# Out product of block 0 by pairs of token groups, and unit 2's and unit 3's attention steps moved ahead by one or two ff tiles

## The chip, the cores and the metric

One core of one Trainium2 chip. The metric is the device time of one execution in microseconds (us). The record calls a time slow when it is over 1.5% above the fastest of its kernel. Times inside an execution are read from its profile; they count from the start of the span, which is about 1.8 us shorter than the device time.

## The reference

Attention inside chunks of 64 tokens (8 batches, 8 heads, 576 tokens, head size 64), then a bilinear feed-forward product on the 4608 tokens that come out:

```python
scores = q_c @ k_c^T / sqrt(64)          # 64 x 64 per chunk and head
attn   = softmax(scores)
x      = (attn @ v_c)  -> [4608, 512]
out    = ((x @ w_a) * (x @ w_b)) @ w_out # d_ff = 1536
```

## The kernel before

The tokens are cut into 9 blocks of 512 and 18 units of 256. A block runs 12 "ff tiles" (eight matmuls into two PSUM banks, the buffers that TensorE writes to, a ScalarE copy, a VectorE product) and then an out product. The attention of the coming units is slipped between the matmuls of the running block: a *turn* (transpose of q and k), *scores*, an exponential, *sums* and values, a logarithm and inverse, and a *normalise* that writes the next block's input `xT`. The banks for the matmuls are a ring of four, `F`; attention uses `PS` and `PA`, of two banks each.

The out product of block 0 holds all four banks of the ring, one for each group of 128 tokens, and carries unit 2's attention:

```python
o = [nextF() for _ in range(4)]
for fts in [(ft,) for ft in range(NFT - 2)] + [(NFT - 2, NFT - 1)]:
    for tg in range(4):
        for ft in fts:
            out_products(tg, ft, o[tg])          # one matmul, N = 512
    if fts == (5,):   # turn of unit 2, on TensorE
        ...           # q evacuated by VectorE, k by ScalarE, both from PS
    if fts == (7,):
        scores(2, True); expo(2)
    if fts == (9,):
        sums(2, SU); values(2); log_sums(2, SU)
        for cl in range(2): inverse(2, cl); normalise(2, cl)
stores = [out_close(0, tg, o[tg], False, (V, A)[tg % 2]) for tg in range(4)]
```

Block 1 follows in two halves of 256 tokens (units 2 and 3). Units 4 and later are turned by a DMA transpose, issued by the sync engine in the order of the program, among loads and stores:

```python
turn_unit(4); load_unit(5, (1, 2))
for d in stores: store(*d)                       # block 0's output
load_unit(6, (0,))
for ft in range(10):                             # block 1, unit 2's half
    step(); ffn(1, ft, (0,))
    if ft == 1: turn_pairs(3, 0, (V,)); turn_pairs(3, 1, (A,))
    if ft == 3: slot(None, 3, True)              # scores of unit 3
    if ft == 5: slot(3, None, short=True)        # sums, ..., normalise of unit 3
cast_unit(5, (0,)); ...                          # GpSimd
turn_unit(5); load_unit(6, (1, 2)); load_unit(7, (0,))
for ft in range(10): step(); ffn(1, ft, (1,)); ...  # unit 3's half
...
for ft in range(10, NFT):
    step(); ffn(1, ft)
    if ft == 10: slot(4, 5)                      # sums of unit 4, scores of unit 5
```

`step()` runs what a slot left for later: exponential, inverse, normalise.

The softmax here doesn't subtract the row's maximum and nothing guards it: scores larger than these inputs give would overflow.

## Time and profile before

| | before |
|---|---|
| device time, median of the first 3 runs | 316.56 us |
| span of the profiled run | 314.3 us |
| TensorE / VectorE / ScalarE / GpSimd busy | 96 / 59 / 43 / 39% |
| first out matmul of block 0 | 37.41 us |
| block 1 starts | 52.34 us |
| scores of unit 5 | 75.55 us |

TensorE is the engine to watch, so what matters is where it stands still. The prediction shows its waits and its timeline. One more view, the busy time of each engine in a stretch of time, shows the hole that the change aims at (columns: the stretch, its length, then busy us and instructions of TensorE, weight loads, VectorE, ScalarE and GpSimd, the granted clock, the DMA share and GB/s):

```profile
50.60:52.30 1.70, 0.00 (x0) 0.00 (x0) 1.70 (x4) 1.25 (x3) 1.48 (x2) 1.00 0.99 223
```

For 1.70 us TensorE runs nothing at all, while VectorE works without a break: block 1 waits for VectorE.

### The profile page before, as it was taken

The page shows a single profiled execution, that of the slowest core. Times are in us where ns is not written, and L with a number is a line of the kernel's source. Part 1 is how long each engine was busy: PE and PEld are TensorE (multiplying, and loading weights), DVE is VectorE, ACT ScalarE, POOL GpSimd, SP SyncE. Part 2 cuts the span into 40 slices and gives each one's busy share as a digit, 9 for nine tenths or more (in the row PEclk, how much of TensorE's full clock was granted, in tenths as well). Part 3 has the DMA queues.
Part 4 walks back from the last instruction along what each step waited for, and adds up shares of the span by engine and source line. Part 5 has one row for each costly group of instructions (what it writes and reads, how often), then busy time and mean ns, then how long its engine had stood idle before and what let it go on. Part 6 is the DMA issues. An engine that isn't in the chain of part 4 may idle for free.

```text
span 314.3 us, 7318 instructions
## 1 busy us (share of the span) xinstructions
PE 300.9 (96%) x2891; PEld 177.9 (57%) x2924; DVE 184.4 (59%) x372; ACT 135.5 (43%) x233; POOL 124.1 (39%) x159
## 2 busy tenths in 40 slices
PE   7699997999999999999999999999999999999995
PEld 3444455876444476447644764467446744674474
DVE  3643314454447764967496749574967476646663
ACT  3822225846335542653265326441644164413320
POOL 2567958996384127402630164016500400040023
PEclk9999999999999999999999999999999999999998
DMA  7999999999999979998699239933500320020003
GB/s 262 267 316 385 372 296 260 218 302 234 224 221 284 228 158 266 238 184 188 198 251 220 68 136 204 265 71 135 134 2 2 84 53 1 2 100 36 0 1 136
DMA packets 146899, 55.01 MB, mean 175 GB/s; under 512 B 126256, under 2 KB 140848, under 8 KB 146864
## 3 DMA queue, kind: packets, MB, share of 16 engines
q1 hardware_dynamic: 145776, 53.49, 69.1%
q10 hardware_dynamic: 1088, 1.05, 1.0%
q8 instruction: 23, 0.38, 0.5%
q14 instruction: 12, 0.10, 0.1%
HBM read 37.75 MB, written 9.44 MB: 150 GB/s over the span
## 4 chain that ended last, share of the span: by engine, by line
PE 87%; DMA 4%; SPq 3%; DVE 2%; issue 1%; ACT 1%; POOL 1%; ACTq 0%; POOLq 0%; DVEq 0%
PE F L398 56%; PE F L479 19%; PE F L420 6%; SPq L154 2%; DMA wst<-in_moe_w_a_dram 2%; PE PS L234 2%; DMA f<-in_k_dram 2%; PE F L251 2%; PE PA L267 1%; SPq L147 1%; DVE xT L286 1%; DVE ab L410 0%; POOL part L497 0%; ACT qkT L167 0%; ACTq L140 0%
## 5 line engine op out<-in xcount | busy, mean ns | idle before, releaser
L398 PE MATMUL F<-xT,wb 128*128 128x512 bf16 (+1 forms) x443 | 110.4, 360 | 4.0 <-DVE osb L169 1.8
L398 PE MATMUL F<-xT,wa 128*128 128x512 bf16 (+1 forms) x472 | 112.9, 361 | 0.7 <-POOL wa L169 0.3
L409 ACT CAST bsb<-F 128x512 bf16<-128x512 f32 (+1 forms) x118 | 64.6, 548 | 106.0 <-PE F L398 105.7
L410 DVE TENSOR_TENSOR ab<-F,bsb 128x512 bf16<-128x512 f32 (+1 forms) x118 | 75.7, 643 | 54.7 <-PE F L398 46.4
L398 PEld LDWEIGHTS <-wa 128*128 128x128 bf16 x472 | 46.0, 98 | 48.2 <-POOL wa L169 1.4
L398 PEld LDWEIGHTS <-wb 128*128 128x128 bf16 x472 | 44.5, 98 | 46.5 <-issue 1.8
L497 POOL TENSOR_TENSOR part<-part 128x256 f32<-128x256 f32 x14 | 10.1, 724 | 133.7 <-ACT part L523 132.8
L169 POOL CAST qkb<-f 128x1024 bf16<-128x1024 f32 (+1 forms) x35 | 34.6, 1003 | 23.4 <-DMA f<-in_k_dram 13.4
L479 PEld LDWEIGHTS <-wst 128*128 128x128 bf16 x420 | 41.1, 98 | 4.8
L286 DVE TENSOR_TENSOR xT<-PA,inv 128x512 bf16<-128x512 f32 x32 | 21.8, 683 | 20.9 <-ACT inv L281 15.2
L479 PE MATMUL F<-wst 128*128 128x256 bf16 x252 | 33.3, 273 | 0.0
L497 DVE TENSOR_TENSOR osb<-F,part 128x256 f32<-128x256 f32 x56 | 22.3, 419 | 10.9 <-POOL part L497 9.4
L497 POOL TENSOR_TENSOR part<-part,osb 128x256 f32<-128x256 f32 x28 | 19.8, 727 | 11.5 <-DVE osb L497 11.4
L169 POOL CAST vb<-f 128x1024 bf16<-128x1024 f32 (+2 forms) x22 | 20.1, 918 | 7.1 <-DMA f<-in_v_dram 6.1
L479 PE MATMUL F<-wst,ab 128*128 128x256 bf16 x168 | 22.7, 273 | 0.0
L420 PE MATMUL F<-wo,ab 128*128 128x512 bf16 x92 | 21.3, 379 | 0.5 <-DVE ab L410 0.2
L468 DVE TENSOR_TENSOR wst<-ab 128x512 bf16<-128x512 bf16 x42 | 21.7, 517 | 0.0
L467 DVE TENSOR_TENSOR wst<-ab 128x512 bf16<-128x512 bf16 x42 | 20.9, 497 | 0.0
L277 ACT ACTIVATE lns<-F 128x512 f32<-128x512 f32 x30 | 16.3, 594 | 10.2 <-PE F L251 10.2
L479 PE MATMUL F<-wo,wst 128*128 128x256 bf16 x168 | 20.6, 273 | 0.0
L245 ACT ACTIVATE E<-PS 128x1024 bf16<-128x1024 f32 (+1 forms) x20 | 18.8, 942 | 3.7 <-PE PS L234 2.5
L497 DVE TENSOR_TENSOR part<-F,part 128x256 f32<-128x256 f32 x15 | 6.4, 425 | 21.3 <-POOL part L497 21.3
(58 smaller groups left out, 194.4 us busy)
## 6 DMA issues: line engine op xcount, KB each, us to landing
out_dram<-osb SPq DMA_DIRECT2D x31, 256.0 KB, 2.1
f<-in_q_dram SPq DMA_DIRECT2D x28, 256.0 KB, 4.3
f<-in_v_dram SPq DMA_DIRECT2D x28, 256.0 KB, 4.3
f<-in_k_dram SPq DMA_DIRECT2D x24, 256.0 KB, 3.9
wst<-in_moe_w_out_dram SPq DMA_DIRECT2D x6, 512.0 KB, 8.8
f<-in_v_dram SPq DMA_DIRECT2D x16, 128.0 KB, 3.3
wst<-in_moe_w_b_dram SPq DMA_DIRECT2D x4, 512.0 KB, 7.4
wst<-in_moe_w_a_dram SPq DMA_DIRECT2D x4, 512.0 KB, 8.2
```

The costliest lines, as they stand in the source:

```text
L169: eng.tensor_copy(out=out, in_=in_)
L245: nc.scalar.activation(out=e[:, :, s], in_=PS[:, :, s], func=AF.Exp, scale=scale)
L277: nc.scalar.activation(out=lns[:, cl, :], in_=SU[cl], func=AF.Ln)
L286: nc.vector.tensor_tensor(out=x.rearrange("p m (g c t) -> p c g m t", g=2, c=2)[:, cl], in0=PA[:, cl, :].rearrange(shape, g=2, m=4), in1=i ...
L398: nc.tensor.matmul(bank[:, 0:n], w[ft // 2][ft % 2][:, kt, :], x[:, kt, us[0] * 256:us[0] * 256 + n], start=(kt == 0), stop=(kt == NKT - 1),)
L409: nc.scalar.copy(out=bT[:, 0:n], in_=banks[0][:, 0:n])
L410: nc.vector.tensor_tensor(out=ab[ft][:, us[0] * 256:us[0] * 256 + n], in0=banks[1][:, 0:n], in1=bT[:, 0:n], op=MULT)
L420: nc.tensor.matmul(o, ab[ft][:, tg * 128:(tg + 1) * 128], wo[ft // 2][:, ft % 2, :], start=(ft == 0), stop=(ft == NFT - 1),)
L467: nc.vector.tensor_tensor(out=y[:, 0:2], in0=a[:, 0:2], in1=a[:, 2:4], op=ADD)
L468: nc.vector.tensor_tensor(out=y[:, 2:4], in0=a[:, 1:3], in1=a[:, 0:4:3], op=SUB)
L479: nc.tensor.matmul(o, a(i)[:, c:c + 128], b(i), start=(i == 0), stop=(i == NP - 1))
L497: eng.tensor_tensor(out=out, in0=in0, in1=in1, op=op)
```

## The change

Its intent is to keep TensorE running from block 0's out product into block 1. The token groups are taken in pairs, so that groups 0 and 1 finish four matmuls ahead of 2 and 3 and can be copied out while these still run; ScalarE now copies the even groups and VectorE the odd ones. Unit 2's turn and scores come 4 matmuls sooner, its sums 8 sooner; unit 3's steps come one ff tile sooner.

```diff
-        for fts in [(ft,) for ft in range(NFT - 2)] + [(NFT - 2, NFT - 1)]:
-            for tg in range(4):
-                for ft in fts:
-                    out_products(tg, ft, o[tg])
-            if fts == (5,):      # turn       (after 24 matmuls)
-            if fts == (7,):      # scores     (after 32)
-            if fts == (9,):      # sums, ...  (after 40)
-        stores = [out_close(0, tg, o[tg], False, (V, A)[tg % 2]) for tg in range(4)]
+        for f0 in range(0, NFT, 2):
+            for tgs in ((0, 1), (2, 3)):
+                for ft in (f0, f0 + 1):
+                    for tg in tgs:
+                        out_products(tg, ft, o[tg])
+                if (f0, tgs[0]) == (4, 0):   # turn       (after 20)
+                if (f0, tgs[0]) == (6, 0):   # scores     (after 28)
+                if (f0, tgs[0]) == (6, 2):   # sums, ...  (after 32)
+        stores = [out_close(0, tg, o[tg], False, (A, V)[tg % 2]) for tg in range(4)]
...
-            if ft == 1:   # turn of unit 3
+            if ft == 0:
-            if ft == 3:   # scores of unit 3
+            if ft == 2:
-            if ft == 5:   # sums of unit 3
+            if ft == 4:
```

(The bodies of the conditions are unchanged and cut here.)

More of the change, by code (lines that the diff above doesn't have):

```diff
@@ L752 @@
         o = [nextF() for _ in range(4)]
-        for fts in [(ft,) for ft in range(NFT - 2)] + [(NFT - 2, NFT - 1)]:
-            for tg in range(4):
-                for ft in fts:
-                    out_products(tg, ft, o[tg])
-            if fts == (5,):
-                t = [transpose_pairs(2, x, PS[:, x, :]) for x in range(2)]
-                evacuate_pairs(2, 0, t[0], (V,))
-                evacuate_pairs(2, 1, t[1], (A,))
-            if fts == (7,):
-                scores(2, True)
-                expo(2)
-            if fts == (9,):
-                SU = PS[:, 0, :], PS[:, 1, :]
-                sums(2, SU)
-                values(2)
-                log_sums(2, SU)
-                for cl in range(2):
-                    inverse(2, cl)
-                    normalise(2, cl)
-        stores = [out_close(0, tg, o[tg], False, (V, A)[tg % 2]) for tg in range(4)]
+        for f0 in range(0, NFT, 2):
[4 more added lines that the diff above has]
+                if (f0, tgs[0]) == (4, 0):
+                    t = [transpose_pairs(2, x, PS[:, x, :]) for x in range(2)]
+                    evacuate_pairs(2, 0, t[0], (V,))
+                    evacuate_pairs(2, 1, t[1], (A,))
+                if (f0, tgs[0]) == (6, 0):
+                    scores(2, True)
+                    expo(2)
+                if (f0, tgs[0]) == (6, 2):
+                    SU = PS[:, 0, :], PS[:, 1, :]
+                    sums(2, SU)
+                    values(2)
+                    log_sums(2, SU)
+                    for cl in range(2):
+                        inverse(2, cl)
+                        normalise(2, cl)
+        stores = [out_close(0, tg, o[tg], False, (A, V)[tg % 2]) for tg in range(4)]
         cast_unit(4, (0,))
```

## The prediction

> **What bounds the kernel now.** I read four views in this order: the page's busy shares, the list of what TensorE waited for, the timeline of the stage that the diff touches, and last the queue of the sync engine.
>
> The page says which engine matters:
>
> ```profile
> PE 300.9 (96%) x2891; PEld 177.9 (57%) x2924; DVE 184.4 (59%) x372; ACT 135.5 (43%) x233; POOL 124.1 (39%) x159
> PEclk9999999999999999999999999999999999999998
> ```
>
> TensorE is busy for 96% of the span at the full granted clock. The change neither adds nor removes a matmul, so all it can win is idle time of TensorE, and 4% of 314.3 us, or 13 us, is all there is, most of it in the start. The waits of TensorE, longest first, say what is within reach:
>
> ```profile
> PE F L398 <- DVE osb L169: 1.8, 1, 1.8
> ...
> PE F L398 <- DVE xT L286: 0.3, 1, 0.3
> ...
> PE F L420 <- DVE ab L410: 0.2, 1, 0.2
> PE PS L234 <- ACT qkT L167: 0.2, 1, 0.2
> ```
>
> The 1.8 us is the first product of block 1 waiting for the first bank of block 0's out product to be copied out. The others lie in the same stage. The timeline of TensorE puts them in place (start, duration, engine, line, operation, count, idle before and releaser):
>
> ```profile
> 37.41 0.81 PE L420 MATMUL F<-wo,ab 128*128 128x512 bf16 x3
> 38.42 4.69 PE L420 MATMUL F<-wo,ab 128*128 128x512 bf16 x20 [0.20 <-DVE ab L410]
> 42.95 1.06 PE L194 MATMUL PS<-identity,qkb 128*128 128x128 bf16 x16
> 43.85 1.89 PE L420 MATMUL F<-wo,ab 128*128 128x512 bf16 x8
> 45.90 0.64 PE L234 MATMUL PS<-qkT 64*64 64x64 bf16 x32 [0.16 <-ACT qkT L167]
> 46.47 1.90 PE L420 MATMUL F<-wo,ab 128*128 128x512 bf16 x7
> 48.30 0.41 PE L251 MATMUL PS<-E,ones 64*64 64x512 bf16 x4
> ...
> 48.90 1.69 PE L420 MATMUL F<-wo,ab 128*128 128x512 bf16 x7
> 52.34 0.60 PE L398 MATMUL F<-xT,wb 128*128 128x256 bf16 x4 [1.76 <-DVE osb L169]
> ```
>
> The reader is to see the out product in pieces of 24, 8, 8 and 8 matmuls with unit 2's attention steps between them, and its hole at the end. The next rows, of VectorE and ScalarE, say why that hole is there:
>
> ```profile
> 49.73 1.15 ACT L281 ACTIVATE inv<-lns 128x512 f32<-128x512 f32 x2
> 50.40 1.29 DVE L286 TENSOR_TENSOR xT<-PA,inv 128x512 bf16<-128x512 f32 x2 [5.66 <-PE F L420]
> 51.60 1.28 DVE L169 COPY osb<-F 128x512 f32<-128x512 f32 x2
> ```
>
> Unit 2's sums come so late that VectorE is still normalising until 51.69; only then does it copy the first bank, although that bank was finished before 50.
>
> **What the Trainium skill says.**
> (1) "TensorE: Matmul & The Clock Gate", Back-to-back issue gap, gives N/2.4 + 2.5 ns, 215.8 ns for N = 512; the same section says that a sustained stream with weight loads reaches about 131 ns. The trace agrees with the first: 35 out matmuls from 81.22 take 7.72 us, (7.72 - 0.38)/34 = 0.216 us. I use 0.216.
> (2) "PSUM — Partial Sum Buffer", Engine vs sequencer instructions: matmuls start and complete in program order. The trace agrees: TensorE sat idle 1.76 us at one blocked matmul. So a step moved forward too far makes everything behind it wait.
> (3) "Perfetto Trace Analysis", Identifying the Most-Contended Engine: matmul busy time is a poor measure of headroom because instructions overlap. The trace agrees: the rows overlap (42.95 starts before 43.11 = 38.42 + 4.69), so I measure losses from start to start and not by the idle column.
> (4) The same page, DMA Instruction — HWDGE: the profiled window ends before the data have moved. The trace agrees: the transpose below is issued for 3.79 us and lands 5.8 us after it began.
>
> **The change part by part.** The number of instructions is the same; their order on TensorE changes. I lay out the new stage from the same start, 37.41.
>
> *Pairs of token groups at the start.* Now the fourth matmul (group 3) needs the bank that the last product of block 0 used, and VectorE frees it only at 38.37. It starts at 38.42 instead of 37.41 + 3 x 0.216 = 38.06: 0.36 us lost. By pairs, groups 2 and 3 first come after four matmuls, at 38.27 and 38.49; their banks are free by then. Gain 0.36.
>
> *Turn of unit 2.* It comes after 20 matmuls, at 37.41 + 20 x 0.216 = 41.73. Its inputs are there: the k part is the last, cast by 41.81 (ScalarE from 41.19 for 0.62), and the eight transposes of q come first and take 0.45. The 16 transposes take 0.90 (42.95 to 43.85), so the out product goes on at 42.63.
>
> *Scores.* Still 8 matmuls behind the turn: 42.63 + 1.73 = 44.36. The evacuations are serial, VectorE then ScalarE, and scores stood 2.95 us after the turn's start (45.90 - 42.95), so they start at 44.68. The loss of 0.32 stays as before (43.85 + 1.73 = 45.58 against 45.90): nothing gained or lost here.
>
> *Sums.* This is where the change pays. They now follow 4 matmuls after scores and not 8. Scores take 0.57 (45.90 to 46.47), 4 matmuls 0.86: TensorE is there at 46.11. The exponential ended 1.70 after scores began (46.58 + 1.02 - 45.90), so it ends at 46.38 and sums start at about 46.43: a new wait of 0.31 us. Before, 46.47 + 8 x 0.216 = 48.20 against 48.30, a loss of 0.10 that this new one replaces.
>
> *The end of the out product.* Sums and values take 0.60 (48.30 to 48.90); then 16 matmuls remain, 3.45 us: 46.43 + 0.60 + 3.45 = 50.48. VectorE ended its normalises 3.39 after sums began (51.69 - 48.30): 49.82. Group 0's last matmul starts at 50.48 - 6 x 0.216 = 49.18 and ends at 49.56; ScalarE, free since 49.01, copies it by about 50.2, before block 1 wants it at 50.48. Group 1 ends about 49.8 and VectorE copies it by 50.5; its bank is wanted 0.44 later. Groups 2 and 3 are copied by 51.1 and 51.4; unit 3's turn wants these banks at 51.35 and 51.8. So the hole closes. Before, the last matmul's successor could have gone at 48.90 + 8 x 0.216 = 50.63 and went at 52.34: 1.71 us gained.
>
> Sum of the stage: 0.36 + 0.10 - 0.31 + 1.71 = 1.86 us, the same as 52.34 - 50.48.
>
> *Block 1, unit 3 one ff tile sooner.* The spacing of turn, scores and sums stays; the run of ff tiles between sums and the first tile of the second half grows from four to five. Before, that tile waited for the last normalise: 63.06 + 0.44 = 63.50 against 63.99, 0.49 us lost. The normalise ends 4.69 us after the sums (63.94 - 59.25); five tiles and the sums' own work take 5 x 0.874 + 0.67 = 5.04. The wait goes: 0.49. Unit 3's k is cast by 50.60, before its turn at 51.35.
>
> So at the end of block 1's halves TensorE is 1.86 + 0.49 = 2.35 us ahead.
>
> *What it then meets.* Units from 4 on are turned by a DMA transpose. That of unit 5 is needed by the scores in the middle of block 1's last tiles:
>
> ```profile
> 68.18 3.79 SPq L216 DMA_TRANSPOSE qkT<-qkb  x1
> DMA to landing us min/median/max: 5.8/5.8/5.8
> 75.55 0.47 PE L234 MATMUL PS<-qkT 64*64 64x64 bf16 x32
> ```
>
> It lands at 68.18 + 5.8 = 73.98. Its queue issues loads, stores and transposes back to back from 56.70 to 72, and the casts ahead wait for DMA, not for TensorE; so it does not come sooner. The scores would now be due at 75.55 - 2.35 = 73.20 and start at about 74.05. The 1.57 us of slack that hid this transfer before is used up and 0.85 us of the gain is given back. Remaining: 2.35 - 0.85 = 1.50 us. Unit 4's transpose (56.70 + 6.5 = 63.2, scores due at 64.4) and unit 8's (99.05 + 5.7 = 104.8, due at 106.65) keep more than a microsecond of slack, and after 75 us TensorE shows no wait worth naming, so 1.50 is carried to the end: 316.56 - 1.50 = 315.06.
>
> **The rivals.**
> A, nothing takes back: all 2.35 us stay, 314.2. For it: no wait of TensorE on a DMA is seen before. Against it: the slack of 1.57 is smaller than the gain.
> B, the new wait at sums is dearer, or the turn meets its cast: the k cast waits for its load (landing near 41.2), and with the turn 1.2 us sooner only some 0.1 to 0.4 us of margin remain. A load late by half a microsecond would cost as much in this stage. But a delay of up to 0.85 here is absorbed by the wait for unit 5's transpose, so the end hardly moves: the transfer is the bound up to 74 us. This makes 315.1 robust from below.
> C, the transpose itself moves: DMA is at or over 100% in this stage, so the landing may vary by half a microsecond either way between builds: 314.5 to 315.6.
> D, unit 3's turn stalls for the banks of groups 2 and 3 (margins of 0.3 to 0.5 us) and ScalarE falls behind: a few tenths, again absorbed at 74.
>
> **Range and chances.** C dominates: 315.1, with 314.3 to 315.9 for 8 in 10, which allows for the spread of the kernel before too (316.37 to 317.33). 2% is 6.3 us, several times everything found here: faster 0.01, within 2% 0.98, slower 0.01.
>
> **What would show it right or wrong.** The TensorE timeline: first four out matmuls without a hole; sums waiting about 0.3 us for the exponential; block 1 starting near 50.5 with the wait on the copy gone; no wait on the normalise near 61.6; and a new wait of about 0.8 us of the scores near 74 for unit 5's transpose. If that wait is absent and the end is 2.3 us sooner, the transfer was not fixed in time; if block 1 starts after 51, the stage's arithmetic is wrong.

## The result, and the profile after

The changed kernel took 315.30 us (median of 4 runs, 314.76 to 315.55) against 316.94 us (median of 4, 316.37 to 317.5). The ratio is 0.9946, 95% interval 0.9921 to 0.9971: faster by about half a per cent, clear of the noise on this chip. Ratios are computed as the mean time of one kernel's fast runs over that of the other's of the same rounds, so they are not quite the ratio of the medians quoted.

The same stretch as above, in the changed kernel, is full:

```profile
50.60:52.30 1.70, 1.70 (x25) 1.61 (x24) 1.30 (x3) 0.91 (x2) 1.04 (x1) 1.00 0.97 220
```

The timeline of TensorE in the changed kernel, the rows that answer to those shown of before:

```profile
37.48 4.48 PE L420 MATMUL F<-wo,ab 128*128 128x512 bf16 x19
41.80 1.06 PE L194 MATMUL PS<-identity,qkb 128*128 128x128 bf16 x16
...
44.74 0.64 PE L234 MATMUL PS<-qkT 64*64 64x64 bf16 x32 [0.16 <-ACT qkT L167]
...
46.51 0.41 PE L251 MATMUL PS<-E,ones 64*64 64x512 bf16 x4 [0.15 <-ACT E L245]
...
50.56 0.60 PE L398 MATMUL F<-xT,wb 128*128 128x256 bf16 x4
...
73.00 0.45 PE L267 MATMUL PA<-E,vb 64*64 64x64 bf16 x32
74.19 0.45 PE L234 MATMUL PS<-qkT 64*64 64x64 bf16 x32 [0.75 <-DMA qkT<-qkb]
```

The hole at the fourth matmul is gone (one piece from 37.48); scores wait as before; sums now wait for the exponential; block 1 starts without a wait. (Counts of 19 and 15 where the program has 20 and 16 are records missing from the trace.) And at 74.19 there is a wait that the kernel before did not have, on the DMA that transposes unit 5. The chain of waits runs through it:

```profile
68.37 5.78 DMA qkT<-qkb
74.15 0.04 issue
74.19 0.45 PE PS L234 x32
```

The transfer lands at 74.15, and the scores start 0.04 us later.

The start of the kernel wanders: over the profiles here the first out matmul lies between 37.10 and 38.48 us. So from here on I count from that matmul, in a table that all experiments share. "Due" is when TensorE had done all that stands ahead of unit 5's scores (the values' start plus 0.27 us, as in undisturbed runs); "landed" is unit 5's transpose, issue plus time to landing; "to unit 9" is the time from the scores of unit 5 to those of unit 9. From unit 9 to the end every run took 189.0 to 189.2 us. Each row is one execution. That of the changed kernel is the fastest of its four, those of e1 and e12 are the fastest of their kernel's six, those of e2 and e6 the slowest, and that of e5 is 0.03 us from the slowest; so a difference between two rows that lies behind unit 5 need not come from the edit.

| run | block 1 starts | scores 5 due | landed | scores 5 start | to unit 9 |
|---|---|---|---|---|---|
| before | 14.93 | 38.14 | 36.6 | 38.14 | 49.69 |
| changed | 13.08 | 35.79 | 36.7 | 36.71 | 49.67 |
| e1, changed, q load behind | 13.08 | 35.78 | 35.1 | 35.78 | 50.36 |
| e2, before, q load behind | 14.92 | 38.13 | 36.3 | 38.13 | 51.29 |
| e3, out product only | 13.08 | 36.29 | 37.6 | 37.67 | 50.48 |
| e4, block 1 only | 14.93 | 37.63 | 38.5 | 38.54 | 50.08 |
| e5, changed, again | 13.08 | 35.93 | 38.8 | 38.81 | 51.10 |
| e6, changed, stores behind | 13.08 | 35.78 | 35.8 | 35.84 | 51.85 |
| e7, changed, k load ahead | 13.07 | 35.78 | 39.7 | 39.71 | 51.28 |
| e8, before, k load ahead | 14.93 | 38.14 | 41.9 | 41.91 | 52.31 |
| e9, changed with room | 13.08 | 35.78 | 34.3 | 35.78 | 50.16 |
| e10, before with room | 14.93 | 38.14 | 34.4 | 38.14 | 49.70 |
| e11, order only | 13.97 | 37.33 | 38.9 | 38.97 | 49.89 |
| e12, e9 and two buffers | 12.85 | 35.56 | 34.3 | 35.56 | 49.86 |

The theory to test: the change brings TensorE 2.35 us ahead, and the transpose of unit 5 takes back what exceeds its slack. The rivals: the wait has another cause; the two parts of the change simply add up; the transfer's place is set by something other than its queue.

All kernels below gave correct results. Three groups of four ran, each on another chip; on these the kernel before took 316.96, 316.74 and 317.18 us (medians of 11) and scattered from 315.7 to 319.4. Whole times separate little there.

### The profile page after: what moved, and what is told of

Read it like the earlier page. It is cut to its first block, busy times and chain, and to the rows that moved or that the text cites.

```text
span 312.9 us, 7317 instructions
## 1 busy us (share of the span) xinstructions
PE 300.5 (96%) x2891; PEld 177.9 (57%) x2924; DVE 186.0 (59%) x372; ACT 135.7 (43%) x233; POOL 124.4 (40%) x159
## 4 chain that ended last, share of the span: by engine, by line
PE 74%; DMA 13%; SPq 5%; POOL 4%; issue 2%; ACTq 0%; POOLq 0%; DVEq 0%; ACT 0%; DVE 0%
PE F L398 47%; PE F L479 19%; DMA f<-in_q_dram 5%; DMA wst<-in_moe_w_a_dram 4%; PE F L420 3%; DMA f<-in_k_dram 3%; SPq L124 2%; DMA qkT<-qkb 2%; PE F L251 1%; PE PS L234 1%; POOL qkb L169 1%; SPq L154 1%; POOL wst L460 1%; PE PA L267 1%; SPq L147 1%
## 5 line engine op out<-in xcount | busy, mean ns | idle before, releaser
L468 DVE TENSOR_TENSOR wst<-ab 128x512 bf16<-128x512 bf16 x42 | 21.4, 509 | 0.0
L467 DVE TENSOR_TENSOR wst<-ab 128x512 bf16<-128x512 bf16 x42 | 21.4, 509 | 0.0
```

The lines of the kernel that those rows point to most:

```text
L467: nc.vector.tensor_tensor(out=y[:, 0:2], in0=a[:, 0:2], in1=a[:, 2:4], op=ADD)
L468: nc.vector.tensor_tensor(out=y[:, 2:4], in0=a[:, 1:3], in1=a[:, 0:4:3], op=SUB)
```

## The experiments

### e1 and e2: unit 6's q load behind the transpose

```diff
         for d in stores: store(*d)
-        load_unit(6, (0,))
...
         turn_unit(5)
-        load_unit(6, (1, 2))
+        load_unit(6)
```

e1 is the changed kernel with it, e2 the kernel before.

> The changed kernel with one edit: unit 6's q load (two issues) is queued behind unit 5's DMA transpose instead of ahead of it. Theory (unit 5's transpose is what takes back 0.9 us): the transpose is issued near 66.3 us instead of 68.37 and lands near 72.1; the scores of unit 5, due at 73.27, wait for nothing (0.75 us idle before), so the end comes 0.9 us sooner than the changed kernel: about 314.4 us, ratio to the kernel before near 0.992. Rival (the wait has another cause, or the next transfer takes its place at once): the scores still start at 74.0 or later, or a wait of the same size appears at the scores of unit 6, and the time stays at 315.3 us.

> The kernel before with the same edit of the queue. Theory (before, the transfer had 1.57 us of slack and bounded nothing): time unchanged within 0.2 us, scores of unit 5 at 75.5 us as before, ratio 1.000. Rival (the queue's order is worth something by itself): 0.5 us or more faster.

e1 took 315.92 us, ratio 0.9975 (0.9941 to 1.0009); e2 317.48 us, ratio 1.0015 (0.9982 to 1.0048). In the table the theory's first half holds to a few hundredths: e1's scores start when due, at 35.78, and e2's are where they were. The full 2.35 us are there at that point (38.13 - 35.78). But the time did not follow. On the way to unit 9, e1 loses 0.67 us and e2 1.60 us against the kernel before. The expectation that nothing else would take the wait's place was wrong, and the rival was right in this: another wait did, although not at the scores of unit 6. (e2's larger loss is read from the slowest of its executions; how much of it the edit makes is not shown.) The list of waits of TensorE between 90 and 112 us, for e2:

```profile
PE F L398 <- DVE ab L410: 1.3, 2, 1.0
```

TensorE waits for VectorE to free a bank. e6 below shows what held VectorE up.

### e3 and e4: the two parts alone

e3 is the changed kernel with block 1's three conditions set back to `ft == 1, 3, 5`; e4 is the kernel before with them at 0, 2, 4.

> Only the out product's part of the change; unit 3's steps in block 1 stay where they were. Theory: block 1 starts near 50.5 us, the normalise of unit 3 still costs its 0.49 us near 62, so the scores of unit 5 are due at 73.7 instead of 73.27, and wait about 0.5 us instead of 0.9: they start at the same 74.1 to 74.2, and the time is that of the whole change, 315.3 us, ratio 0.995. Rival (the two parts add up in the time): 0.5 us slower than the whole change, 315.8 us.

> Only block 1's part: unit 3's turn, scores and sums one ff tile sooner, the out product as before. Theory: block 1 still starts at 52.3 us, the wait on unit 3's normalise (0.49 us) is gone, and since 1.57 us of slack lies ahead of unit 5's transpose, all of it stays: 0.5 us faster than before, 316.4 us, ratio 0.9985, scores of unit 5 at 75.05. Rival (the part is worth nothing by itself, it only serves the whole): same as before, scores at 75.5.

e3 took 316.62 us, ratio 0.9993 (0.9950 to 1.0035); e4 317.36 us, ratio 1.0003 (0.9966 to 1.0041). TensorE's own part came as computed: due at 36.29 in e3 (1.85 us ahead of before) and 37.63 in e4 (0.51 ahead). The transfer did not: it landed 1 us later than in the first profiles in e3 and 1.9 later in e4, so both waited, e3 for 1.38 us where I expected 0.5, e4 for 0.91 where I expected none. The two parts are worth 1.85 and 0.51 us up to the transfer. What is left of them behind it depends on when it lands, and that moves by more than I had thought. The times themselves decide nothing here: both intervals hold the expected ratios (0.995 and 0.9985) as well as 1.

### e5: the changed kernel again

> The changed kernel unaltered, run again as the control of this group. Theory: scores of unit 5 due 35.8 us after the out product begins, and waiting for unit 5's transpose, which lands 36.6 to 37.7 us after it; ratio to before 0.995. Rival (the wait was an accident of the one profile): no wait there, the scores start 35.8 us after the out product begins.

It took 316.53 us, ratio 0.9981 (0.9948 to 1.0014) on this chip: here the change can't be told from no change. The wait is there again, larger: landed at 38.8, 2.9 us after the scores were due. And the wait cost more than its length. Windows around it (columns as above; the granted clock is the number before the last two):

```profile
72.00:74.00 2.00, 1.21 (x39) 0.58 (x37) 0.69 (x1) 1.38 (x3) 1.81 (x3) 1.00 1.24 230
74.00:76.00 2.00, 0.09 (x8) 0.09 (x12) 0.69 (x1) 1.12 (x2) 1.97 (x3) 0.90 0.95 216
76.00:78.00 2.00, 2.00 (x36) 1.01 (x37) 0.00 (x0) 0.00 (x0) 0.97 (x1) 0.50 1.14 261
78.00:80.00 2.00, 2.00 (x8) 0.79 (x7) 0.29 (x1) 1.51 (x2) 1.49 (x2) 0.75 0.98 217
80.00:82.00 2.00, 2.00 (x11) 0.78 (x8) 1.00 (x2) 0.00 (x0) 1.66 (x3) 1.00 0.84 192
```

TensorE is busy for all of 76 to 78, but the clock was granted at half, and only 8 matmuls fit between 78 and 80 where 11 do between 80 and 82. From the scores of unit 5 to those of unit 6 this run took 16.45 us against 15.04 in the kernel before, 1.4 us more. The Trainium skill, "TensorE: Matmul & The Clock Gate", What's actually happening, has the clock fall to half after an idle window of about 3.4 us that runs freely. The trace agrees on the window: the clock fell at 75.60, before the wait had ended, and stayed down for 3.41 us. It does not agree on idle: in the 3.41 us up to 75.60 TensorE had been busy for 1.02. Nor does the length of a wait decide it. Waits of 0.75 us (the first profile of the changed kernel), 1.20 (e3), 1.5 (e11) and 1.76 (before) left the clock alone, yet in the start of e2, e3, e4, e7 and e8 it fell for 3.41 us although no wait just ahead was longer than 0.94 us. In e3:

```profile
10.07:13.48 3.41, 2.03 (x77) 1.45 (x74) 1.85 (x5) 3.14 (x5) 2.15 (x6) 1.00 1.06 256
13.48:16.90 3.42, 3.42 (x37) 1.49 (x38) 1.63 (x3) 2.34 (x4) 1.84 (x3) 0.50 1.05 304
```

What the window measures is not shown: after the kernel before was busy for only 1.65 of the 3.41 us from 49.80, its clock stayed full.

This run also says what the change is worth when the transfer is as late as this. The kernel before needs it at 38.14; landing at 38.8, it would make that kernel wait too, and the two would start the scores together. That is worked out and not run. In these profiles e5 took 278.94 us from the first out matmul to the end and the kernel before 276.86, so a late transfer can cost more than the change wins.

### e6: the stores behind the transpose

```diff
-        for d in stores: store(*d)
         load_unit(6, (0,))
...
         turn_unit(5)
+        for d in stores: store(*d)
```

> The changed kernel with the four stores of block 0 queued behind unit 5's transpose, unit 6's q load left ahead of it. Theory (the queue's order sets when the transpose goes out): it is issued about 2.4 us sooner, right after unit 5's k is cast near 65.9 us, lands near 71.8, and the scores of unit 5 wait for nothing: they start 35.8 us after the out product begins instead of 36.7. GpSimd's casts of unit 6 come sooner, not later, so the stall of VectorE against GpSimd that the earlier edit showed near 97 us (0.3 us of TensorE) is not there; 0.9 us faster than the changed kernel, ratio to before near 0.992. Rival (the transfer's slot is taken by data movement, not by the queue's order): it lands at 73.5 us or later and the scores still wait.

315.69 us, ratio 0.9959 (0.9928 to 0.9990). The scores start at 35.84, 0.06 after they are due. Against e5, on the same chip, the transfer is issued 2.75 us sooner (30.72 after the first out matmul, against 33.47) and lands 3.0 us sooner, which speaks for the queue's order and against the rival of this run. Against the first profile of the changed kernel it is issued only 0.17 us sooner (30.89), so with one profile of each the size of the effect is not settled. The second half of the expectation was a miss. The loss behind is not gone but larger, 2.16 us to unit 9. VectorE in e6, where it forms block 2's sums of products (L466 to L468, bf16 from two operands in SBUF):

```profile
96.79 0.79 DVE L466 TENSOR_TENSOR wst<-ab 128x256 bf16<-128x256 bf16 x1
97.50 1.25 DVE L467 TENSOR_TENSOR wst<-ab 128x512 bf16<-128x512 bf16 x1
98.68 1.25 DVE L468 TENSOR_TENSOR wst<-ab 128x512 bf16<-128x512 bf16 x1
```

and GpSimd beside it:

```profile
95.17 2.27 POOL L460 TENSOR_TENSOR wst<-wst 128x256 bf16<-128x256 f32 x3
97.38 2.28 POOL L169 CAST qkb<-f 128x1024 bf16<-128x1024 f32 x2
```

Later in e6, with GpSimd idle, the same L467 and L468 take 0.42 us each. The Trainium skill, "SBUF — State Buffer", Who interferes with whom, states that a VectorE instruction with two SBUF inputs contends with a GpSimd instruction that reads SBUF, and the second waits for the first. The trace agrees: 1.25 us beside GpSimd's casts, 0.42 alone, and the two slow ones end 0.28 and 0.27 us after the cast beside them (98.48 to 98.76, 99.66 to 99.93). GpSimd is at this work so late because it takes the casts of unit 7 in order and stood idle for 4.58 us ahead of unit 7's k, whose load had not landed; the weight sums stood in line behind it.

### e7 and e8: a load more ahead of the transpose

```diff
-        load_unit(6, (0,))
+        load_unit(6, (0, 1))       # q and k ahead of turn_unit(5)
```

> The changed kernel with unit 6's k load (two issues, 1.2 us) also queued ahead of unit 5's transpose. Theory: no slack is left there, so the delay of 1.2 us appears in full: the scores wait about 2.0 us instead of 0.75 and start 37.9 us after the out product begins instead of 36.7; 1.2 us slower than the changed kernel, ratio to before near 0.999. Rival (the transposes are not the bound): unchanged at 0.995.

> The kernel before with the same delay. Theory: its 1.57 us of slack take up the 1.2 us, scores of unit 5 at 38.1 us after the out product begins as before, with no wait or one under 0.3 us; ratio 1.000. Rival (the delay costs the same wherever it falls): 1.2 us slower, ratio 1.004.

e7 took 320.54 us, ratio 1.0104 (1.0071 to 1.0136); e8 321.67 us (median of its three fast runs), ratio 1.0133 (1.0081 to 1.0185). The direction of e7 is the theory's; its size, and e8 altogether, missed, because the dose was not what I wrote. I had taken 1.2 us from an issue of two k loads that met an empty queue; here these two issues took 3.28 us in e7 and 3.50 us in e8, and the transposes landed at 39.7 and 41.9. That is past what even the kernel before could hide, so e8 does not test its slack. The longest wait, in e7:

```profile
78.19 0.59 PE L234 MATMUL PS<-qkT 64*64 64x64 bf16 x32 [3.76 <-DMA qkT<-qkb]
```

What the pair does show: the scores start 0.04 to 0.05 us after the landing in both, whatever TensorE had gained ahead of it, and the waits of 3.8 and 3.6 us again halved the clock, for 1.6 and 2.6 us more to unit 6.

### e9 and e10: room for the change

```diff
 # the stores behind turn_unit(5), as in e6, and
-        cast_unit(7, (0, 1))
+        cast_unit(7, (0,))
+        some_sums(24)
+        cast_unit(7, (1,))
...
-        some_sums(24)              # was behind cast_unit(7, (2,))
```

e9 is the changed kernel with both edits, e10 the kernel before with both.

> The changed kernel with room made behind it: the four stores queued behind unit 5's transpose, and the last sums of the output weights on GpSimd done before it waits for unit 7's k instead of after unit 7's v. Theory (two things take back what the change wins: unit 5's transpose, and VectorE's sums of block 2 slowed to 0.9 to 1.3 us by GpSimd's sums beside them): the scores of unit 5 start 35.8 us after the out product begins, from there to the scores of unit 9 it is 49.7 us (51.85 with the stores moved alone), so the end is 2.3 us sooner than an undisturbed run before: 314.3 us, ratio 0.991 or less. Rival (the stall of VectorE comes from the stores or from block 2 itself): still 51 us or more from the scores of unit 5 to those of unit 9.

> The kernel before with the same two edits. Theory: it had slack ahead of the transpose, so its scores of unit 5 stay at 38.1 us after the out product begins; only the later stall of VectorE can be saved, 0 to 0.6 us on this chip; ratio 0.998 to 1.000. The change is then worth the full 2.35 us between this run and the one above it, instead of 1.4. Rival (the room helps both alike): ratio 0.994 or less.

e9 took 314.89 us, ratio 0.9930 (0.9902 to 0.9959); e10 316.47 us, ratio 0.9985 (0.9956 to 1.0015). At the scores of unit 5 the two differ by 2.36 us (38.14 - 35.78): with room, the change is worth all that was computed for it there. The scores of unit 5 in e9 wait for nothing:

```profile
73.58 0.47 PE L234 MATMUL PS<-qkT 64*64 64x64 bf16 x32
```

VectorE in e9, at the work that took 1.25 us in e6:

```profile
95.26 0.29 DVE L466 TENSOR_TENSOR wst<-ab 128x256 bf16<-128x256 bf16 x1
95.47 0.41 DVE L467 TENSOR_TENSOR wst<-ab 128x512 bf16<-128x512 bf16 x1
95.81 0.42 DVE L468 TENSOR_TENSOR wst<-ab 128x512 bf16<-128x512 bf16 x1
```

To unit 9 it took 50.16 us where I expected 49.7. Most of this loss has a wait of its own, again a DMA transpose, now that of unit 8:

```profile
106.67 0.44 PE L234 MATMUL PS<-qkT 64*64 64x64 bf16 x32 [0.31 <-DMA qkT<-qkb]
```

So 1.90 us of the 2.36 are left at unit 9 (35.78 + 50.16 = 85.94 against 38.14 + 49.70 = 87.84). In time the two medians differ by 1.58 us. e9 has the lowest ratio to before, but its interval overlaps that of the changed kernel (0.9921 to 0.9971) and that kernel was not run in this group, so what the room adds to the change in time is not shown. e10, with the same room and without the change, did not leave 1 by more than its interval.

### e11: the order alone

The loop and the copies of the change, with the turn, scores and sums still after 24, 32 and 40 matmuls and block 1 as before.

> Only the order by pairs of token groups and the swapped copies at the end; unit 2's steps stay after 24, 32 and 40 matmuls, block 1 as before. Theory: the hole at the fourth matmul goes (0.36 us); the sums come 10.5 us after the out product begins, VectorE normalises until 13.9, and block 1's first product, which reads what it wrote, starts there: 13.95 us after the out product begins, against 14.93 before and 13.08 with the whole change. So about 1.0 of the stage's 1.86 us come from the order and 0.9 from the earlier steps. Rival (the order alone closes the hole): 13.1 us. Rival (the order alone does nothing at the end): 14.6 us.

317.12 us, ratio 1.0000 (0.9965 to 1.0035). Block 1 starts at 13.97, 0.02 from the expectation, and both rivals fall (13.1 and 14.6). The row of TensorE names what is left:

```profile
51.77 0.61 PE L398 MATMUL F<-xT,wb 128*128 128x256 bf16 x4 [1.16 <-DVE xT L286]
```

It waits now for the normalise, no longer for the copy. Of the 1.85 us of the stage, the order, with the swapped copies, gives 0.96 and the earlier steps 0.89. The swap was not run by itself. The time shows none of it: the transpose landed at 38.9, and the scores waited for it.

### e12: two buffers for the turn

```diff
-        t = [transpose_pairs(2, x, PS[:, x, :]) for x in range(2)]
+        t = [transpose_pairs(2, x, (PA, PS)[x][:, x, :]) for x in range(2)]
```

on top of e9.

> As the changed kernel with room, and unit 2's q is transposed into the other two-bank buffer, so that VectorE and ScalarE need not take turns at one buffer when they evacuate it. Theory (they take turns because both read the same buffer): ScalarE starts as soon as k's transposes are done, scores follow the 8 matmuls without the 0.32 us of waiting, and everything behind is 0.3 us sooner: block 1 starts 12.75 us after the out product begins instead of 13.08. Rival (the order of the two copies has another cause): scores still 2.95 us after the turn begins.

315.45 us, ratio 0.9950 (0.9917 to 0.9983), not to be told from e9 in time. In the trace ScalarE's evacuation no longer waits for VectorE's. First e9, then e12:

```profile
43.93 1.07 ACT L167 COPY qkT<-PS 128x512 bf16<-128x512 bf16 x2 [2.82 <-DVE qkT L169]
```

```profile
43.35 1.07 ACT L167 COPY qkT<-PS 128x512 bf16<-128x512 bf16 x2 [2.01 <-PE PS L194]
```

In e12 its releaser is TensorE, and it starts at 43.35, while VectorE's copy runs from 42.90 to 43.59. The shared buffer was the cause of the turn-taking. The semaphores in the traces say who asks for it: in e9 the copy waits on the one that VectorE's copy counts up, in e12 on one of TensorE's. So it is the program that makes ScalarE wait. Scores begin 2.72 us after the turn instead of 2.95, block 1 at 12.85 instead of 13.08: 0.23 us of the expected 0.32.

## Why the prediction was right

Predicted 315.1 us with a range of 314.3 to 315.9; measured 315.30 us.

- *Start of the out product, 0.36 us.* Right: no hole, the turn 4.32 us after the first matmul; 20 x 0.216 is 4.32.
- *Turn and scores, nothing gained.* Right: scores start 2.94 us after the turn, with the same 0.16 us of idle.
- *Sums, a new wait of 0.31 us.* Right from start to start: the sums start 9.03 us after the first matmul, where 46.43 - 37.41 = 9.02 was predicted. The idle column shows 0.15 us of it.
- *End of the out product, 1.71 us.* Right: block 1 starts at 13.08, where 50.48 - 37.41 = 13.07 was predicted. e11 splits the stage's gain: half is the order with the swapped copies, half the earlier steps.
- *Unit 3 one tile sooner, 0.49 us.* Right: no wait on the normalise; e4 has 0.51 us of it alone.
- *Unit 5's transpose takes back 0.85 us.* Right in cause and nearly in size: 0.92 us (36.71 - 35.79). In e1, e6 and e9 the transfer landed sooner and the wait went (0.06 us are left in e6); in e3, e4, e5, e7, e8 and e11 they start less than 0.1 us behind the landing.
- *1.50 us carried to the end.* Right between these two profiles: 276.86 us from the first out matmul to the end before, 275.40 after, 1.46 us.

Rival A (all 2.35 us stay) fell: even with e9's room 1.90 us are left at unit 9. Rivals B and D (the earlier steps meet their inputs, unit 3's turn meets its banks) did not occur: block 1 starts at 13.07 or 13.08 in all seven runs that have the out product part as the change has it, and unit 3's turn, at 51.44 in the changed kernel, shows no wait.

What was too narrow is rival C. I allowed the landing half a microsecond either way; in the kernels whose queue was not altered it lies between 36.6 and 38.9. That scatter is as large as the gain, and e5's 316.53 us, on another chip, lies outside my range. That the time came within 0.3 us of the prediction is therefore in part luck: the first two profiles have the earliest landings of the six. And "after 75 us TensorE shows no wait worth naming" held for the two first profiles only: on slower loads the sums of VectorE meet GpSimd's work near 97 us.

What stays open: why the loads are slower in some runs and on some chips. Where they are, the queue of the sync engine, GpSimd and VectorE are all late together. Open too is how much of the losses behind unit 5 in e1, e2 and e6 the edits make.

## What to carry to other kernels

Before closing a hole in the bounding engine, list the next transfers and buffers that it will meet and subtract its gain from the slack of each; here 2.35 us of gain met 1.57 us of slack. Then make room with the order in the DMA queue and of the off-path engine's work: what is not urgent (stores, sums that wait for no load) goes behind or into an idle stretch. And profile more than once, since the slack ahead of a transfer is a property of a run and not of the kernel.

## What the Trainium skill lacked or had wrong

- "TensorE: Matmul & The Clock Gate", Back-to-back issue gap: about 131 ns for each N = 512 matmul in a sustained stream with weight loads is not seen here. 35 out matmuls, each with its own weight load, came at 216 ns, the figure that the page gives for an isolated matmul.
- The same page, What's actually happening: an idle window of about 3.4 us before the clock halves. Here the clock halved after windows of 3.41 us that were not idle: TensorE was busy for 1.02 us in e5 (1.4 us lost) and for 2.03 in the start of e3, with no wait over 0.94 us. A window with 1.65 busy (before, from 49.80) left it full. A reader who stays under 3.4 us is not yet safe, and no run here gives a safe length.
- "SBUF — State Buffer", Who interferes with whom: right, and worth a number for bf16 sums: 0.42 us alone, 1.25 us beside GpSimd's casts.
- "Perfetto Trace Analysis", DMA Instruction — HWDGE: it says that the transfer is not in the profiled window, but not how far the window itself stretches. The same two k loads were issued in 1.20 us (after the changed kernel's transpose of unit 5) and in 3.28 us (e7), so an issue time is no fixed cost.
- On no page that I read: two engines that copied from different banks of one two-bank PSUM buffer took turns here, which cost 0.23 us of TensorE (e9 against e12). It is a semaphore wait in the program; whether the chip would need it for two banks of one buffer, no run here shows.
